# Linformer attention and maxout FFN: batch 0 loaded by casting DMAs of one queue, first FFN chunk begun with half of the features

## Chip, cores, metric

One core of a Trainium2 chip. The metric is device time in microseconds (us). "Span" is the time from the first to the last instruction in a profile or a timed execution. It is 2.1 to 2.2 us shorter than the time for the kernel before and about 1.8 us shorter for the changed one. I compare times with times and spans with spans.

In the profile lines PE is TensorE, PEld its weight loads, DVE is VectorE, ACT ScalarE, POOL GpSimd, SP the engine that issues the plain loads. A timeline line gives start and duration in us, the engine, the line of the kernel, the tiles written and read with their shapes, and the count; in brackets stands how long the engine was idle before it and what ended that wait. The granted clock is TensorE's clock as a share of full speed.

## The reference, cut to what matters

```python
k_proj = einsum('ks,bhsd->bhkd', E, k);  v_proj = einsum('ks,bhsd->bhkd', F, v)
attn   = softmax(q @ k_proj.T / 8)               # b=8 batches, 8 heads, s=1024, d=64, k=64
x      = (attn @ v_proj) -> [8192, 512]          # heads side by side
h      = max(x @ w1, x @ w2, x @ w3)             # 512 -> 768
out    = h @ w_out                               # 768 -> 512
```

All inputs are fp32 in HBM; the kernel computes in bf16 with fp32 sums.

## The kernel before

Heads go in four pairs ("pair g"). Each pair of batch 0 gives 128 of the 512 features of x. The FFN runs in chunks of 512 tokens. TensorE's order is fixed by the program; `bank()` and `two()` deal one PSUM bank or two neighbouring ones of eight, the one that the program's own clock thinks free first; `idle(n)` issues filler matmuls.

Batch 0 comes as fp32 over the SP queue, is cast on DVE and ACT, and the weights follow on the GpSimd queue, held back by casts:

```python
    load_q(0); load_k(0); load_k(1); load_q(1)                # nc.sync, fp32 tiles q_f, k_f
    for (a, b), t in zip([(0, 4), (4, 6), (6, 8)], v_f):
        nc.sync.dma_start(out=t, in_=view(v, 0)[:, a:b])
    ...
    cast_k(2, "v")
    load_w(0, 0, cast_k(3, "v"))                              # w1, features 0-255, after this cast
    ...                                                       # (cut: pairs 0 to 3)
    cast_v(2, "v"); cast_v(3, "s")
    v_pair(1)
    scale_x(0, 0, *C0, values(0, 0, *C0))
    ...
    v_pair(3)
    idle(1)
```

The first FFN chunk keeps six sums of w1 in six PSUM banks, then takes w2 and w3:

```python
        for i in range(3):
            ...
            if i == 0:    # features 0-127 of all six, 128-255, then 256-511; pair 3's values inside
                parts = [(A, (0,)), (Bq, (0,)), (A, (1,)), (Bq, (1,)), (A, (2, 3)), (Bq, (2, 3))]
            else:
                parts = [(A, (0, 1)), (A, (2, 3)), (Bq, (0, 1)), (Bq, (2, 3))]
            ...
                        if i == 0:
                            copy("sv"[jt % 2], hs[:, jt], t, ns)          # w1 to SBUF
                        else:
                            most(hs[:, jt] if i == 1 else hTs[0, 0][:, jt, :], t, ns, hs[:, jt])
```

The softmax here doesn't subtract the row's maximum and nothing guards it: scores larger than these inputs give would overflow.

Of the kernel before, what the change touches and what calls it, by code (L numbers as in the profile page):

```python
# [15 lines left out]
def kernel(  # L16
# [21 lines left out]
    P = 128  # L38
# [98 lines left out]
    first_ctx = ExitStack()  # L137
    first = first_ctx.enter_context(tc.tile_pool(name="first", bufs=1))

    ef_f = first.tile([P, S], FP32, name="ef_f")  # L140
    ef_b = first.tile([P, S], BF16, name="ef_b")
    q_f = [first.tile([P, 4, SPC, D], FP32, name=f"q_f{i}") for i in range(2)]
    k_f = [first.tile([P, 4, SI, D], FP32, name=f"k_f{i}") for i in range(2)]
    k_c = [first.tile([P, SI, 2, D], BF16, name=f"k_c{g}") for g in range(NPAIR)]
    q_c = [first.tile([P, 2, SPC, 2, D], BF16, name=f"q_c{i}") for i in range(2)]
    v_heads = [(0, 4), (4, 6), (6, 8)]
    v_f = [first.tile([P, b - a, SI, D], FP32, name=f"v_f{a}") for a, b in v_heads]
# [3 lines left out]
    def load_q(i):  # L151
        nc.sync.dma_start(out=q_f[i], in_=view(q, 0)[:, 4 * i:4 * i + 4, 0:SPC])  # L152

    def load_k(i):
        nc.sync.dma_start(out=k_f[i], in_=view(k, 0)[:, 4 * i:4 * i + 4])

    load_q(0)
    load_k(0)
    load_k(1)
    load_q(1)  # L160
    for (a, b), t in zip(v_heads, v_f):
        nc.sync.dma_start(out=t, in_=view(v, 0)[:, a:b])  # L162
# [6 lines left out]
    def load_w(i, half, earlier=None):  # L169
        cts = slice(half * NCT // 2, (half + 1) * NCT // 2)  # L170
        w = (moe_w1, moe_w2, moe_w3)[i].rearrange("(ct p) j -> p ct j", p=P)
        dma = nc.gpsimd.dma_start(out=w_sb[i][:, cts, :], in_=w[:, cts, :])
        if earlier is not None:
            after(dma, earlier)

    def load(b):
        tiles = tuple(
            loads.tile([P, H, SI, D], BF16, name=nm) for nm in ("q_t", "k_t", "v_t")
        )
        qkv[b] = tiles  # L180
        for i in ((1, 0, 2) if b == 1 else (0, 1, 2)):
            dma = nc.gpsimd.dma_start(out=tiles[i], in_=view((q, k, v)[i], b))  # L182
            if i == 0 and b - 1 in last_T:
                after(dma, last_T[b - 1])



# [140 lines left out]
    LO, HI = slice(0, H // 2), slice(H // 2, H)  # L328

# [63 lines left out]
    def cast_q(g, eng):  # L393
        copy(
            eng, q_c[g // 2][:, g % 2].rearrange("p si h d -> p h si d"),
            q_f[g // 2][:, 2 * (g % 2):2 * (g % 2) + 2],
        )

    def turn_q(g):
        t, ns = two()  # L400
        t = t.bitcast(BF16)[:, 0]
        for si in range(SPC):
            nc.tensor.transpose(
                out=t[:, si * P:(si + 1) * P],
                in_=q_c[g // 2][:, g % 2, si].rearrange("p h d -> p (h d)"),
                identity=ident,
            )
        pe(0.3)
        copy(
            "v", qTs[0][:, g * SI:g * SI + SPC, :].rearrange("a si p -> a (si p)"),  # L410
            t[:, 0:CHUNK], ns, 0.43,
        )

    def cast_k(g, eng):
        return copy(
            eng, k_c[g].rearrange("p si h d -> p h si d"),
            k_f[g // 2][:, 2 * (g % 2):2 * (g % 2) + 2], (), 0.7,
        )

    def k_pair(g):  # L420

        t, ns = bank()
        for si in range(SI):
            nc.tensor.matmul(
                out=t[:, 0:KP], lhsT=k_c[g][:, si].rearrange("p h d -> p (h d)"),
                rhs=efT[:, si, 0, :], start=(si == 0), stop=(si == SI - 1),
            )
        pe(0.5)
        copy("v", kpTs[0][:, g, :], t[:, 0:KP], ns, 0.25)

    def cast_v(g, eng):
        a = (0, 0, 4, 6)[g]
        return copy(
            eng, v_t[:, 2 * g:2 * g + 2],
            v_f[max(0, g - 1)][:, 2 * g - a:2 * g - a + 2], (), 0.7,
        )
# [6 lines left out]

    C0 = (0, SPC)
    idle(11)
    turn_ef()
    cast_q(0, "v")
    cast_q(1, "s")
    idle(3)
    turn_q(0)  # L450
    turn_q(1)
    idle(6)
    cast_k(0, "v")
    cast_k(1, "s")
    k_pair(0)
    idle(1)
    k_pair(1)
    sc01 = [scores(0, 0, *C0)]
    exps(0, 0, *C0, sc01[0])
    idle(1)  # L460
    sc01.append(scores(0, 1, *C0))
    exps(0, 1, *C0, sc01[1])
    idle(1)
    z01 = [sums(0, 0, *C0)]
    idle(1)
    invert(0, 0, *C0, z01[0])
    cast_k(2, "v")
    load_w(0, 0, cast_k(3, "v"))
    k_pair(2)
    z01.append(sums(0, 1, *C0))  # L470
    invert(0, 1, *C0, z01[1])
    cast_q(2, "v")
    k_pair(3)
    cast_q(3, "v")
    turn_q(2)
    turn_q(3)
    sc23 = [scores(0, g, *C0) for g in (2, 3)]
    for g in (2, 3):
        exps(0, g, *C0, sc23[g - 2])
    idle(3)  # L480
    load_w(0, 1, cast_v(0, "v"))
    load_w(1, 0)
    load_w(1, 1)
    load_w(2, 0)
# [41 lines left out]
    def up_first(work):  # L526
# [5 lines left out]
        for i in range(3):  # L532
# [8 lines left out]
            for n, (jts, cts) in enumerate(parts):  # L541
                for jt in jts:
                    if h[jt] is None:
                        h[jt] = bank()
# [200 lines left out]
```

## Time and profile before

| | before |
|---|---|
| time, first runs | 408.73, 408.83, 408.86 and 410.6 us |
| span of the profiled execution | 409.1 us, mean granted clock 0.994 |
| TensorE busy | 395.4 us, 97% |
| first FFN matmul | 23.74 us |
| first matmul of the down projection | 43.04 us |

TensorE is the bound from about 25 us on. The interesting part is the head: what TensorE waits for until then. I use the first down matmul as a mark; everything ahead of it is "the head". The prediction shows the lines.

### The profile page before, as it was taken

What the parts mean: (1) busy time and instruction counts of PE and PEld (TensorE: products, weight loads), DVE (VectorE), ACT (ScalarE), POOL (GpSimd) and SP (SyncE); (2) the same over time, 40 slices, a digit from 0 to 9 for tenths busy, and PEclk for the clock granted to TensorE, in tenths of its full rate; (3) what the DMA queues carried; (4) which work ended last, traced back from release to release, by engine and by line L of the source; (5) the groups of instructions that cost most, each with busy time, mean ns of one, the idle gap of its engine ahead of it and who ended that gap; (6) DMA issues with size and microseconds to landing.
All of it is one profiled execution on the core that took longest, in us unless ns stands there. A gap on an engine that the chain in (4) does not pass through costs nothing.

```text
span 409.1 us, 6066 instructions
## 1 busy us (share of the span) xinstructions
PE 395.4 (97%) x2415; PEld 181.1 (44%) x2459; DVE 205.8 (50%) x319; ACT 194.2 (47%) x281; POOL 25.3 (6%) x35
## 2 busy tenths in 40 slices
PE   7889999999999999999999999999999999999995
PEld 3534444345444544444544445444544444444443
DVE  2737655464474526636463564525465363525251
ACT  3721527722764266457435555536545556432322
POOL 0421002002000200200110002000000000000000
PEclk9989999999999999999999999999999999999999
DMA  8999948958935994596699108970440202020202
GB/s 263 353 207 204 183 132 123 229 154 123 244 55 129 211 229 128 87 226 124 183 185 198 53 0 225 200 194 0 66 142 2 103 0 104 0 105 0 104 0 103
DMA packets 58475, 54.91 MB, mean 134 GB/s; under 512 B 25936, under 2 KB 52048, under 8 KB 58448
## 3 DMA queue, kind: packets, MB, share of 16 engines
q0 software_dynamic: 25296, 25.69, 39.4%
q1 hardware_dynamic: 33008, 28.71, 21.6%
q8 instruction: 19, 0.31, 0.3%
q10 hardware_dynamic: 144, 0.13, 0.1%
q14 instruction: 8, 0.07, 0.1%
HBM read 57.15 MB, written 16.78 MB: 181 GB/s over the span
## 4 chain that ended last, share of the span: by engine, by line
PE 90%; DMA 4%; SPq 2%; ACT 1%; issue 1%; DVE 1%; DVEq 0%
PE banks L513 60%; PE banks L611 19%; PE banks L216 4%; PE banks L277 3%; DMA v_f<-in_v_dram 3%; PE banks L196 2%; SPq L162 1%; PE banks L288 1%; DMA out_dram<-o_sb 0%; DVE m L576 0%; DVE xT L246 0%; ACT o_sb L99 0%; SPq L152 0%; ACT zi L235 0%; ACT v_t L99 0%
## 5 line engine op out<-in xcount | busy, mean ns | idle before, releaser
L513 PE MATMUL banks<-xT,w_sb 128*128 128x512 bf16 x1118 | 254.7, 380 | 2.1 <-issue 0.6
L513 PEld LDWEIGHTS <-w_sb 128*128 128x128 bf16 x1152 | 109.9, 98 | 137.6 <-issue 10.9
L576 DVE TENSOR_TENSOR m<-banks,h1s 128x512 f32<-128x512 f32 x90 | 62.1, 690 | 86.3 <-ACT h1s L572 54.7
L572 ACT COPY h1s<-banks 128x512 f32<-128x512 f32 x90 | 52.5, 583 | 92.8 <-PE banks L513 89.6
L611 PE MATMUL banks<-wout_sb,hT 128*128 128x512 bf16 x370 | 84.8, 379 | 0.9 <-issue 0.3
L246 DVE TENSOR_TENSOR xT<-banks,zi 128x1024 bf16<-128x1024 f32 (+1 forms) x36 | 39.7, 1106 | 77.2 <-ACT zi L235 57.4
L523 DVE TENSOR_TENSOR hT<-banks,m 128x512 bf16<-128x512 f32 x90 | 62.3, 692 | 9.4
L99 ACT COPY o_sb<-banks 128x512 f32<-128x512 f32 (+1 forms) x60 | 34.9, 581 | 53.0 <-PE banks L611 53.0
L611 PEld LDWEIGHTS <-hT 128*128 128x128 bf16 x378 | 36.1, 98 | 45.5 <-DVE hT L523 2.9
L229 ACT ACTIVATE zl<-banks 128x1024 f32<-128x1024 f32 (+1 forms) x36 | 33.5, 930 | 31.7 <-PE banks L216 31.6
L207 ACT ACTIVATE pT<-banks 128x1024 bf16<-128x1024 f32 (+1 forms) x36 | 33.4, 932 | 9.9 <-PE banks L196 9.0
L235 ACT ACTIVATE zi<-zl 128x1024 f32<-128x1024 f32 (+1 forms) x36 | 34.6, 962 | 1.1
L182 POOL DMA_DIRECT2D q_t<-in_q_dram x7 | 6.2, 880 | 208.9 <-DMA qT<-q_p 61.5
L277 PEld LDWEIGHTS <-efT 128*64 128x64 bf16 x288 | 14.0, 113 | 5.2 <-issue 4.7
L216 PE MATMUL banks<-pT,ones 64*64 64x512 bf16 (+1 forms) x144 | 13.9, 376 | 0.8 <-DVE xT L246 0.3
L196 PE MATMUL banks<-qT,kpT 64*64 64x512 bf16 (+1 forms) x144 | 13.4, 360 | 0.9 <-DVE m L576 0.3
L216 PE MATMUL banks<-pT,vp 64*64 64x512 bf16 (+1 forms) x144 | 13.4, 359 | 0.2 <-DVE vp L99 0.2
L277 PE MATMUL banks<-v_t,efT 128*64 128x256 bf16 (+1 forms) x176 | 10.3, 262 | 2.0 <-ACT v_t L99 2.0
L372 PE MATMUL banks<-warm 128*128 128x512 bf16 x29 | 10.1, 469 | 1.2 <-DVE warm L165 1.2
L216 PEld LDWEIGHTS <-ones 64*64 64x64 bf16 x144 | 4.3, 103 | 14.9 <-issue 14.7
L99 DVE CAST vp<-banks 64x256 bf16<-64x256 f32 (+1 forms) x18 | 7.1, 396 | 6.0 <-ACT vp L99 3.4
L99 ACT CAST vp<-banks 64x256 bf16<-64x256 f32 x14 | 5.1, 365 | 7.3 <-PE banks L277 7.1
(50 smaller groups left out, 104.5 us busy)
## 6 DMA issues: line engine op xcount, KB each, us to landing
out_dram<-o_sb SPq DMA_DIRECT2D x30, 512.0 KB, 3.6
k_t<-in_k_dram POOLq DMA_DIRECT2D x7, 1024.0 KB, 14.5
q_t<-in_q_dram POOLq DMA_DIRECT2D x7, 1024.0 KB, 9.4
v_t<-in_v_dram POOLq DMA_DIRECT2D x7, 1024.0 KB, 18.6
w_sb<-in_moe_w_dram POOLq DMA_DIRECT2D x6, 384.0 KB, 8.5
k_f<-in_k_dram SPq DMA_DIRECT2D x2, 1024.0 KB, 7.9
q_f<-in_q_dram SPq DMA_DIRECT2D x2, 512.0 KB, 7.2
v_f<-in_v_dram SPq DMA_DIRECT2D x1, 1024.0 KB, 11.6
```

Of the source, the lines that this page charges most:

```text
L99: done = {"v": nc.vector.tensor_copy, "s": nc.scalar.copy, "g": nc.gpsimd.tensor_copy}[eng](out=o, in_=i)
L207: nc.scalar.activation(out=pTs[b, g, lo], in_=t, func=AF.Exp, scale=scale)
L216: nc.tensor.matmul(out=t[hp * HALF:(hp + 1) * HALF, c, 0:nsi * HALF], lhsT=w(rows, hp), rhs=p[rows, hp, :], start=True, stop=True,)
L229: nc.scalar.activation(out=zl, in_=t, func=AF.Ln)
L235: nc.scalar.activation(out=zi, in_=zl, func=AF.Exp, scale=-1.0)
L246: nc.vector.tensor_tensor(out=xTs[b][:, g, lo:lo + nsi, :].rearrange("a (c s) p -> a c (s p)", c=2), in0=t, in1=zi, op=ALU.mult,)
L277: nc.tensor.matmul(out=t[hh * HALF:(hh + 1) * HALF, 0:width], lhsT=efT[:, si, kv - 1, :], rhs=qkv[b][kv][:, heads[hh], si, :], start=(si = ...
L513: nc.tensor.matmul(out=h, lhsT=w_sb[i][:, ct, jt * P:(jt + 1) * P], rhs=xTs[b][:, ct, ch * SPC:(ch + 1) * SPC, :], start=(ct == 0), stop=( ...
L523: nc.vector.tensor_tensor(out=o, in0=h, in1=other, op=ALU.max)
L572: nc.scalar.copy(out=h1s, in_=h[0][0])
L576: nc.vector.tensor_tensor(out=m12, in0=h[1][0], in1=h1s, op=ALU.max)
L611: nc.tensor.matmul(out=o_ps, lhsT=hTs[b, ch][:, jt, tt * P:(tt + 1) * P], rhs=wout_sb[:, jt, :], start=(jt == 0), stop=(jt == NJT - 1),)
```

## The change

The intent is to start the FFN earlier. All of batch 0 comes as bf16 through casting DMAs of the GpSimd queue, nearly in the order of need, so the casts go. When only pairs 0 and 1 are done, the FFN begins with features 0 to 255: w1's half sums are copied to SBUF (s1), w2's half sums stay open in six PSUM banks. Pairs 2 and 3 are computed as one "duo" in between. Then come the second halves; w1's is added to s1 on GpSimd.

```diff
-    load_q(0); load_k(0); load_k(1); load_q(1)      # nc.sync, fp32, then casts
+    load_q(LO, slice(0, SPC)); load_kv(1, LO)       # nc.gpsimd, fp32 -> bf16
+    load_kv(2, slice(0, 2));   load_kv(2, slice(2, 4))
+    load_w(0, 0)
+    load_q(HI, slice(0, SPC)); load_kv(1, HI)
+    load_w(1, 0)
+    load_kv(2, V2); load_kv(2, V3)
+    load_w(1, 1); load_w(0, 1); load_w(2, 0); load_w(2, 1)
 ...
+        h = six()
+        for ct in range(2):
+            for jt in jts:
+                up_mm(h[jt][0], 0, 0, 0, jt, (ct,), last=1)      # w1, features 0-255
+                if ct == 1:
+                    copy("sv"[jt % 2], s1[:, jt], *h[jt])
+        then(0)                                                 # q, k, exp, sums of pairs 2, 3
+        load_k1()
+        h = six()
+        for ct in range(2):
+            for jt in jts:
+                up_mm(h[jt][0], 1, 0, 0, jt, (ct,))             # w2, features 0-255, stay in PSUM
+        then(2)                    # v_pair(2), x_pairs(1, (0,)), v_pair(3), x_pairs(1, (1,))
+        for jt in jts:
+            t, ns = bank()
+            up_mm(t, 0, 0, 0, jt, (2, 3), first=2)
+            copy("s", s2[:, jt], t, ns)
+            nc.gpsimd.tensor_tensor(out=s1[:, jt], in0=s1[:, jt], in1=s2[:, jt], op=ALU.add)
+            up_mm(h[jt][0], 1, 0, 0, jt, (2, 3))
+            most(s1[:, jt], *h[jt], s1[:, jt], added)
+        for jt in jts:
+            ...                                                 # w3, all features, then max into hT
 ... (cut: duo versions of transposes, scores, exp, sums, values; plan of the work between)
```

More of the change, by code (lines that the diff above doesn't have):

```diff
@@ L135, with load_kv, load_q, load_w @@
     qkv[0] = (q_t, k_t, v_t)
-    first_ctx = ExitStack()
-    first = first_ctx.enter_context(tc.tile_pool(name="first", bufs=1))
-    ef_f = first.tile([P, S], FP32, name="ef_f")
-    ef_b = first.tile([P, S], BF16, name="ef_b")
-    q_f = [first.tile([P, 4, SPC, D], FP32, name=f"q_f{i}") for i in range(2)]
-    k_f = [first.tile([P, 4, SI, D], FP32, name=f"k_f{i}") for i in range(2)]
-    k_c = [first.tile([P, SI, 2, D], BF16, name=f"k_c{g}") for g in range(NPAIR)]
-    q_c = [first.tile([P, 2, SPC, 2, D], BF16, name=f"q_c{i}") for i in range(2)]
-    v_heads = [(0, 4), (4, 6), (6, 8)]
-    v_f = [first.tile([P, b - a, SI, D], FP32, name=f"v_f{a}") for a, b in v_heads]
+    ef_f = const.tile([P, S], FP32, name="ef_f")
+    ef_b = const.tile([P, S], BF16, name="ef_b")
     nc.sync.dma_start(out=ef_f[0:KP], in_=E)
     nc.sync.dma_start(out=ef_f[KP:P], in_=F)
-    def load_q(i):
-        nc.sync.dma_start(out=q_f[i], in_=view(q, 0)[:, 4 * i:4 * i + 4, 0:SPC])
-    def load_k(i):
-        nc.sync.dma_start(out=k_f[i], in_=view(k, 0)[:, 4 * i:4 * i + 4])
-    load_q(0)
-    load_k(0)
-    load_k(1)
-    load_q(1)
-    for (a, b), t in zip(v_heads, v_f):
-        nc.sync.dma_start(out=t, in_=view(v, 0)[:, a:b])
+    def load_kv(i, heads):
+        nc.gpsimd.dma_start(
+            out=qkv[0][i][:, heads], in_=view((q, k, v)[i], 0)[:, heads]
+        )
+    def load_q(heads, sis):
+        nc.gpsimd.dma_start(
+            out=q_t[:, heads, sis], in_=view(q, 0)[:, heads, sis]
+        )
+    def load_w(i, half):
+        cts = slice(half * NCT // 2, (half + 1) * NCT // 2)
+        w = (moe_w1, moe_w2, moe_w3)[i].rearrange("(ct p) j -> p ct j", p=P)
+        nc.gpsimd.dma_start(out=w_sb[i][:, cts, :], in_=w[:, cts, :])
+    LO, HI, ALL = slice(0, H // 2), slice(H // 2, H), slice(0, H)
+    V2, V3 = slice(4, 6), slice(6, 8)
+    load_q(LO, slice(0, SPC))
+    load_kv(1, LO)
+    load_kv(2, slice(0, 2))
+    load_kv(2, slice(2, 4))
     nc.scalar.preload_act_table_set("natural_log_exp_and_others")
@@ L167, with load_k1 @@
     nc.vector.memset(ones, 1.0)
-    def load_w(i, half, earlier=None):
-        cts = slice(half * NCT // 2, (half + 1) * NCT // 2)
-        w = (moe_w1, moe_w2, moe_w3)[i].rearrange("(ct p) j -> p ct j", p=P)
-        dma = nc.gpsimd.dma_start(out=w_sb[i][:, cts, :], in_=w[:, cts, :])
-        if earlier is not None:
-            after(dma, earlier)
+    load_w(0, 0)
+    load_q(HI, slice(0, SPC))
+    load_kv(1, HI)
+    load_w(1, 0)
+    load_kv(2, V2)
+    load_kv(2, V3)
+    load_w(1, 1)
+    load_w(0, 1)
+    load_w(2, 0)
+    load_w(2, 1)
+    load_q(ALL, slice(SPC, SI))
+    nc.gpsimd.dma_start(out=wout_sb, in_=moe_w_out.rearrange("(jt p) m -> p jt m", p=P))
+    def load_k1():
+        nonlocal k_t1
+        k_t1 = loads.tile([P, H, SI, D], BF16, name="k_t")
+        nc.gpsimd.dma_start(out=k_t1, in_=view(k, 1))
+    k_t1 = None
     def load(b):
         tiles = tuple(
-            loads.tile([P, H, SI, D], BF16, name=nm) for nm in ("q_t", "k_t", "v_t")
+            loads.tile([P, H, SI, D], BF16, name=nm) if b > 1 or i != 1 else k_t1
+            for i, nm in enumerate(("q_t", "k_t", "v_t"))
         )
         qkv[b] = tiles
-        for i in ((1, 0, 2) if b == 1 else (0, 1, 2)):
+        for i in ((0, 2) if b == 1 else (0, 1, 2)):
             dma = nc.gpsimd.dma_start(out=tiles[i], in_=view((q, k, v)[i], b))
@@ L327 @@
     kps = {}
-    LO, HI = slice(0, H // 2), slice(H // 2, H)
     def kproj(b):
@@ L391, in turn_ef @@
             )
-    def cast_q(g, eng):
-        copy(
-            eng, q_c[g // 2][:, g % 2].rearrange("p si h d -> p h si d"),
-            q_f[g // 2][:, 2 * (g % 2):2 * (g % 2) + 2],
-        )
-    def turn_q(g):
-        t, ns = two()
-        t = t.bitcast(BF16)[:, 0]
-        for si in range(SPC):
-            nc.tensor.transpose(
-                out=t[:, si * P:(si + 1) * P],
-                in_=q_c[g // 2][:, g % 2, si].rearrange("p h d -> p (h d)"),
-                identity=ident,
-            )
-        pe(0.3)
-        copy(
-            "v", qTs[0][:, g * SI:g * SI + SPC, :].rearrange("a si p -> a (si p)"),
-            t[:, 0:CHUNK], ns, 0.43,
-        )
-    def cast_k(g, eng):
-        return copy(
-            eng, k_c[g].rearrange("p si h d -> p h si d"),
-            k_f[g // 2][:, 2 * (g % 2):2 * (g % 2) + 2], (), 0.7,
-        )
     def k_pair(g):
@@ L423, in k_pair @@
         for si in range(SI):
-            nc.tensor.matmul(
-                out=t[:, 0:KP], lhsT=k_c[g][:, si].rearrange("p h d -> p (h d)"),
-                rhs=efT[:, si, 0, :], start=(si == 0), stop=(si == SI - 1),
-            )
-        pe(0.5)
-        copy("v", kpTs[0][:, g, :], t[:, 0:KP], ns, 0.25)
-    def cast_v(g, eng):
-        a = (0, 0, 4, 6)[g]
-        return copy(
-            eng, v_t[:, 2 * g:2 * g + 2],
-            v_f[max(0, g - 1)][:, 2 * g - a:2 * g - a + 2], (), 0.7,
-        )
+            for hp in range(2):
+                nc.tensor.matmul(
+                    out=t[hp * HALF:(hp + 1) * HALF, 0:KP],
+                    lhsT=k_t[:, 2 * g + hp, si, :],
+                    rhs=efT[:, si, 0, :], start=(si == 0), stop=(si == SI - 1),
+                )
+        pe(0.45)
+        copy("v", kpTs[0][:, g, :], t[:, 0:KP], ns, 0.25)
     def v_pair(g):
@@ L442, in v_pair, with q_duo @@
         copy("v", vps[0][:, hs].rearrange("a h d -> a (h d)"), t[:, 0:2 * D], ns, 0.3)
+    def q_duo(u):
+        t, ns = bank()
+        t = t.bitcast(BF16)
+        for gg in range(2):
+            heads_q(0, 2 * u + gg, range(SPC), t[:, gg * CHUNK:(gg + 1) * CHUNK])
+        o = qTs[0].rearrange("a (g si) p -> a g si p", si=SI)
+        copy(
+            "v", o[:, 2 * u:2 * u + 2, 0:SPC, :],
+            t.rearrange("a (g si p) -> a g si p", si=SPC, p=P), ns, 0.7,
+        )
+    N0 = SPC * HALF
@@ new lines, in sc_duo @@
+    def sc_duo(u):
+        t, ns = two()
+        for gg in range(2):
+            g = 2 * u + gg
+            for c in range(2):
+                for hp in range(2):
+                    rows = slice(hp * HALF, (hp + 1) * HALF)
+                    at = g * SI + c * SPC // 2
+                    nc.tensor.matmul(
+                        out=t[c * HALF:(c + 1) * HALF, hp, gg * N0:(gg + 1) * N0],
+                        lhsT=kpTs[0][rows, g, :],
+                        rhs=qTs[0][rows, at:at + SPC // 2, :],
+                        start=True, stop=True,
+                    )
+        return t, ns, pe(0.5)
@@ new lines, in exp_duo, with sum_duo @@
+    def exp_duo(u, sc):
+        t, ns, ready = sc
+        pTs[0, u] = att.tile([P, 2, CHUNK], BF16, name="pT", bufs=4)
+        nc.scalar.activation(out=pTs[0, u], in_=t, func=AF.Exp, scale=scale)
+        runs("s", ready, 1.0, ns)
+    def sum_duo(u):
+        t, ns = two()
+        for c in range(2):
+            rows = slice(c * HALF, (c + 1) * HALF)
+            for hp in range(2):
+                nc.tensor.matmul(
+                    out=t[hp * HALF:(hp + 1) * HALF, c],
+                    lhsT=ones[rows], rhs=pTs[0, u][rows, hp, :],
+                    start=True, stop=True,
+                )
+        ready = pe(0.25)
+        zl = att.tile([P, 2, CHUNK], FP32, name="zl", bufs=1)
+        nc.scalar.activation(out=zl, in_=t, func=AF.Ln)
+        runs("s", ready, 1.0, ns)
+        zi = att.tile([P, 2, CHUNK], FP32, name="zi", bufs=2)
+        nc.scalar.activation(out=zi, in_=zl, func=AF.Exp, scale=-1.0)
+        zis[0, u] = zi, runs("s", ready, 1.0)
@@ new lines, in x_pairs @@
+    def x_pairs(u, pairs):
+        t, ns = two()
+        for i, gg in enumerate(pairs):
+            for c in range(2):
+                rows = slice(c * HALF, (c + 1) * HALF)
+                for hp in range(2):
+                    nc.tensor.matmul(
+                        out=t[hp * HALF:(hp + 1) * HALF, c, i * N0:(i + 1) * N0],
+                        lhsT=vps[0][rows, 2 * (2 * u + gg) + hp, :],
+                        rhs=pTs[0, u][rows, hp, gg * N0:(gg + 1) * N0],
+                        start=True, stop=True,
+                    )
+        ready = pe(0.15 * len(pairs))
+        zi, when = zis[0, u]
+        for i, gg in enumerate(pairs):
+            g = 2 * u + gg
+            nc.vector.tensor_tensor(
+                out=xTs[0][:, g, 0:SPC, :].rearrange("a (c s) p -> a c (s p)", c=2),
+                in0=t[:, :, i * N0:(i + 1) * N0],
+                in1=zi[:, :, gg * N0:(gg + 1) * N0],
+                op=ALU.mult,
+            )
+            runs("v", max(ready, when), 0.69, ns)
@@ L446, with up_mm @@
     turn_ef()
-    cast_q(0, "v")
-    cast_q(1, "s")
-    idle(3)
-    turn_q(0)
-    turn_q(1)
+    q_duo(0)
     idle(6)
-    cast_k(0, "v")
-    cast_k(1, "s")
     k_pair(0)
-    idle(1)
-    k_pair(1)
-    sc01 = [scores(0, 0, *C0)]
-    exps(0, 0, *C0, sc01[0])
-    idle(1)
-    sc01.append(scores(0, 1, *C0))
-    exps(0, 1, *C0, sc01[1])
-    idle(1)
-    z01 = [sums(0, 0, *C0)]
-    idle(1)
-    invert(0, 0, *C0, z01[0])
-    cast_k(2, "v")
-    load_w(0, 0, cast_k(3, "v"))
-    k_pair(2)
-    z01.append(sums(0, 1, *C0))
-    invert(0, 1, *C0, z01[1])
-    cast_q(2, "v")
-    k_pair(3)
-    cast_q(3, "v")
-    turn_q(2)
-    turn_q(3)
-    sc23 = [scores(0, g, *C0) for g in (2, 3)]
-    for g in (2, 3):
-        exps(0, g, *C0, sc23[g - 2])
-    idle(3)
-    load_w(0, 1, cast_v(0, "v"))
-    load_w(1, 0)
-    load_w(1, 1)
-    load_w(2, 0)
-    nc.gpsimd.dma_start(out=q_t[:, :, SPC:], in_=view(q, 0)[:, :, SPC:])
-    load_w(2, 1)
-    nc.gpsimd.dma_start(out=wout_sb, in_=moe_w_out.rearrange("(jt p) m -> p jt m", p=P))
-    cast_v(1, "v")
-    z23 = [sums(0, 2, *C0)]
-    invert(0, 2, *C0, z23[0])
-    v_pair(0)
-    z23.append(sums(0, 3, *C0))
-    invert(0, 3, *C0, z23[1])
-    cast_v(2, "v")
-    cast_v(3, "s")
-    v_pair(1)
-    scale_x(0, 0, *C0, values(0, 0, *C0))
-    idle(1)
-    scale_x(0, 1, *C0, values(0, 1, *C0))
-    v_pair(2)
-    idle(2)
-    scale_x(0, 2, *C0, values(0, 2, *C0))
-    v_pair(3)
-    idle(1)
-    first_ctx.close()
+    k_pair(1)
+    for g in range(2):
+        exps(0, g, *C0, scores(0, g, *C0))
+    z01 = []
+    for g in range(2):
+        idle(2)
+        z01.append(sums(0, g, *C0))
+        invert(0, g, *C0, z01[g])
+        v_pair(g)
+    idle(1)
+    for g in range(2):
+        scale_x(0, g, *C0, values(0, g, *C0))
     ffn_sb = ctx.enter_context(tc.tile_pool(name="ffn_sb", bufs=2))
     hTs = {}
-    def up_mm(h, i, b, ch, jt, cts):
+    def up_mm(h, i, b, ch, jt, cts, first=0, last=NCT - 1):
         for ct in cts:
@@ L516, in up_mm @@
                 rhs=xTs[b][:, ct, ch * SPC:(ch + 1) * SPC, :],
-                start=(ct == 0),
-                stop=(ct == NCT - 1),
+                start=(ct == first),
+                stop=(ct == last),
             )
@@ L526, in up_first @@
     def up_first(work):
-        hs = ffn_sb.tile([P, NJT, CHUNK], FP32, name="hs", bufs=1)
-        hTs[0, 0] = ffn_sb.tile([P, NJT, CHUNK], BF16, name="hT")
-        A, Bq = (0, 1, 2), (3, 4, 5)
-        for i in range(3):
-            if i == 0:
-                h = [(t[:, n], ns[n:n + 1]) for t, ns in (two(), two(), two()) for n in (0, 1)]
-            else:
-                h = [None] * NJT
-            if i == 0:
-                parts = [(A, (0,)), (Bq, (0,)), (A, (1,)), (Bq, (1,)), (A, (2, 3)), (Bq, (2, 3))]
-            else:
-                parts = [(A, (0, 1)), (A, (2, 3)), (Bq, (0, 1)), (Bq, (2, 3))]
-            for n, (jts, cts) in enumerate(parts):
-                for jt in jts:
-                    if h[jt] is None:
-                        h[jt] = bank()
-                    up_mm(h[jt][0], i, 0, 0, jt, cts)
-                    if cts[-1] == NCT - 1:
-                        t, ns = h[jt]
-                        if i == 0:
-                            copy("sv"[jt % 2], hs[:, jt], t, ns)
-                        else:
-                            most(
-                                hs[:, jt] if i == 1 else hTs[0, 0][:, jt, :], t, ns, hs[:, jt]
-                            )
-                run_later()
-                for f in work.get((i, n), []):
-                    f()
@@ new lines, in then, with six @@
+        def then(key):
+            run_later()
+            for f in work.get(key, []):
+                f()
+        s1 = ffn_sb.tile([P, NJT, CHUNK], FP32, name="s1", bufs=1)
+        s2 = ffn_sb.tile([P, NJT, CHUNK], FP32, name="s2", bufs=1)
+        hTs[0, 0] = ffn_sb.tile([P, NJT, CHUNK], BF16, name="hT")
+        jts = range(NJT)
+        def six():
+            return [(t[:, n], ns[n:n + 1]) for t, ns in (two(), two(), two()) for n in (0, 1)]
+        h = six()
[4 more added lines that the diff above has]
+                    copy("sv"[jt % 2], s1[:, jt], *h[jt])
@@ new lines, in up_first @@
+        then(0)
[6 more added lines that the diff above has]
+        for jt in jts:
+            t, ns = bank()
+            up_mm(t, 0, 0, 0, jt, (2, 3), first=2)
+            copy("s", s2[:, jt], t, ns)
+            nc.gpsimd.tensor_tensor(out=s1[:, jt], in0=s1[:, jt], in1=s2[:, jt], op=ALU.add)
+            added = clock["s"] + 1.2
+            up_mm(h[jt][0], 1, 0, 0, jt, (2, 3))
+            most(s1[:, jt], *h[jt], s1[:, jt], added)
@@ L558, in up @@
+        then(4)
+        for jt in jts:
+            t, ns = bank()
+            up_mm(t, 2, 0, 0, jt, range(NCT))
+            most(hTs[0, 0][:, jt, :], t, ns, s1[:, jt])
+            then(5 + jt)
     def up(b, ch, jt):
@@ L698, with attend @@
                 c1 = (SPC, SPC)
+                def attend(u):
+                    exp_duo(u, sc_duo(u))
                 up_first({
-                    (0, 0): [lambda: scale_x(0, 3, *C0, values(0, 3, *C0))],
-                    (1, 3): [qp(0, (0, 1), *c1)],
-                    (2, 0): [qp(0, (2, 3), *c1), sc(0, 0, *c1)],
-                    (2, 1): [sc(0, 1, *c1)],
-                    (2, 3): [za(0, 0, *c1), sc(0, 2, *c1)],
+                    0: [lambda: q_duo(1), lambda: k_pair(2), lambda: k_pair(3),
+                        lambda: attend(1), lambda: idle(3), lambda: sum_duo(1)],
+                    2: [lambda: v_pair(2), lambda: x_pairs(1, (0,)),
+                        lambda: v_pair(3), lambda: x_pairs(1, (1,))],
+                    5: [qp(0, (0, 1), *c1)],
+                    6: [qp(0, (2, 3), *c1)],
+                    7: [sc(0, 0, *c1)],
+                    8: [sc(0, 1, *c1)],
+                    10: [za(0, 0, *c1), sc(0, 2, *c1)],
                 })
```

## The prediction

> **What bounds the kernel now.** I read the page's 40 slices first: TensorE is busy nine tenths or more nearly everywhere, so a gain must come out of slots where it is busy with filler or waiting. Then the windows, to see which slots these are.
>
> ```profile
> 0.00:5.00 5.00, 3.81 (x9) 1.34 (x10) 0.35 (x2) 1.28 (x1) 0.70 (x6) 1.00 0.58 134
> 5.00:10.00 5.00, 3.71 (x27) 1.85 (x26) 2.47 (x6) 2.23 (x4) 0.00 (x0) 1.00 1.06 386
> 10.00:15.00 5.00, 4.45 (x65) 2.62 (x64) 3.38 (x11) 4.06 (x7) 0.88 (x1) 1.00 1.06 395
> 15.00:20.00 5.00, 4.52 (x77) 2.44 (x74) 4.27 (x9) 3.70 (x7) 3.05 (x5) 1.00 1.10 325
> 20.00:25.00 5.00, 2.96 (x24) 1.47 (x24) 0.98 (x2) 1.04 (x1) 3.14 (x4) 0.72 1.15 209
> 25.00:30.00 5.00, 5.00 (x26) 2.23 (x26) 1.97 (x3) 1.32 (x3) 0.00 (x0) 0.94 1.30 202
> 30.00:35.00 5.00, 4.95 (x24) 2.25 (x23) 3.09 (x6) 0.43 (x1) 0.00 (x0) 1.00 1.22 208
> ...
> 50.00:409.00 359.00, 351.35 (x2046) 160.54 (x2084) 178.87 (x267) 173.08 (x248) 15.78 (x18) 1.00 0.55 119
> ```
>
> Columns: stretch, its length, busy time of PE, PEld, DVE, ACT, POOL, then granted clock, DMA share, GB/s. From 25 us on PE is full, and stays so (351 of 359 us after 50); in 20 to 25 it is busy 2.96 of 5 us, and the clock falls to 0.72. Then the chain of work that ended last:
>
> ```profile
> 8.44 12.79 DMA v_f<-in_v_dram
> 21.23 0.02 issue
> 21.25 1.05 ACT v_t L99
> 22.30 0.04 issue
> 22.34 1.06 PE banks L277 x16
> 23.41 0.54 PE banks L372
> 23.95 1.28 PE banks L513 x3
> ```
>
> Everything hangs on the last piece of v (heads 6 and 7), which lands at 21.2 us; then a cast, its projection, and the first FFN matmul at 23.74. From there the chain is PE alone to the end. So this is two problems: a head of some 25 us set by loads and by dependent small steps, and 384 us of PE work, which the change hardly touches. The timeline gives the mark to compare with: the first down matmul starts at 43.04.
>
> ```profile
> 43.04 1.46 PE L611 MATMUL banks<-wout_sb,hT 128*128 128x512 bf16 x6
> ```
>
> **What the Trainium skill says.** (1) "DMA: Bandwidth & Descriptors", section "Issuing engines are not separate DMA queues": all queues share the same 16 engines, so a cast on another queue is not free bandwidth. The trace agrees: with v still loading, the third v piece took 12.8 us once weights went in beside it. (2) "GPSIMD Engine Reference", section 3.1: a fp32 tensor_tensor add of 2048 elements measured 4497 ns on GpSimd, about 2.6 cycles an element. For 512 elements that is an estimate of 1.1 to 1.2 us; no such add runs in this trace (the DVE's of that size take 690 ns). (3) "SBUF — State Buffer", section "Who interferes with whom": a DVE instruction with one SBUF input does not contend with GpSimd. The DVE maxima here read PSUM and one SBUF tile, so I charge nothing; this trace cannot show it. (4) "TensorE: Matmul & The Clock Gate", Part 1: idle windows of about 3.4 us halve the clock. The trace has such a drop (0.72) around the 2.01 us wait before 22.34.
>
> **The change, part by part.**
>
> *Loads.* Fp32 loads moved about 400 GB/s (windows); casting loads write about 208 GB/s of bf16, which is 416 GB/s read. Per input element they cost the same, so the total DMA time does not shrink; the order changes. Counting fp32 bytes read (E and F 0.52 MB, q low heads 0.52, k low 1.05, v pairs 0.52 each, a half weight 0.79), before had k's first half in at 9.42 us (issue 2.62 plus 6.8) after 2.1 MB. After needs the same 2.1 MB for it. The software queue starts slower (an isolated q load at 93.55 took 9.3 us for what is 5.0 us at rate), but it starts beside E and F, which ran at 218 GB/s only. I take 9.4 us for k low and 0.416 MB per 1 us onwards: w1 first half about 14 us, k high 18, w2 first half 20, v4-5 and v6-7 21.4 and 22.6, w2 second half 24.5, w1 second half 26.4, w3 28 to 30, wout 36.5. The built program makes the ninth software DMA wait for the first to land, the tenth for the second; seven stay outstanding, so I charge nothing.
>
> *Casts removed.* Twelve casts on DVE and ACT go (q 0.42, k and v 0.69 each on DVE, 1.05 on ACT); with them the wait cast-then-PE ahead of k, q and v.
>
> *Chain from k low to the first FFN matmul.* Two k projections of 16 small matmuls, 0.55 each as an estimate from the v projection's 0.57 to 0.64; kpT copy 0.23; scores 0.25; two exps 0.59; sums; ln 0.60 and exp 0.63 twice; the scale 0.69: k pair from 9.45, exp at 10.9 to 12.1, ln and inverse of pair 0 to 13.4, of pair 1 to 14.7, xT pair 0 ready 15.3. First FFN matmul about 15.4 instead of 23.74; its 12 matmuls (220 ns each in the steady rows) end at 18.0.
>
> *Pairs 2 and 3 inside the FFN.* q transposes 0.6, the qT copy 0.69 behind three DVE copies of s1 (ready 19.9), scores, one exp of 1.04, sums: PE gets to w2 at 22.3 and ends it at 24.95. Then v pair 2, its copy, values, scale, and only then v pair 3: the open w2 sums hold six banks, so all four share the last two banks, and the built program shows v pair 3 and the first w1 matmul waiting for DVE. Each round is 0.64 + 0.35 + 0.30 + 0.80 = 2.1 us, of which PE works 0.9; the second w1 half starts at 29.05. About 2.4 us of new PE wait.
>
> *The add and the maxima.* w1 and w2 second halves: 24 matmuls, 5.3 us, to 34.3. Each s1+s2 goes PE, ACT copy 0.59, GpSimd add 1.2, DVE max 0.69. First add starts at 30.2, the sixth ends at 37.4, the DVE max at 38.1. DVE then does hT and qT (0.69 each, in order), so the scores of chunk 1 get qT at 39.5, while PE could be there at 38.1: 1.4 us of wait. After them come 0.3 + 0.9 + 0.3 + 1.8 + 0.7 us of matmuls: down starts near 43.5.
>
> *Sum.* 43.5 against 43.04: +0.5 us. The 8.3 us won at the start of the FFN go to pairs 2 and 3 (some 6 us with their own waits, formerly ahead of the FFN), the bank round (2.4) and the add chain (1.4); the cold stretch at 22 to 25 us, about 1.3 us by its longer matmuls, is saved. What follows is the same matmuls.
>
> **The rivals.**
>
> A: loads set the head. If software DMAs start 1 us later than I take, k low lands at 10.4 and all of it moves: 410.3. For it: the isolated load's slow start. Against: weights issued at 16.95 landed in 6.8 us beside others. If they start earlier (two queues at once), 408.3.
>
> B: no new waits. If the bank round and the add chain hide better, PE is the bound from 15.4 on; 3.8 us come back: 405.5. Against: the order of the built program shows the waits.
>
> C: the GpSimd add is slower, 1.6 us in place of 1.2: six adds are 2.4 us later, and DVE passes it all on: 411.7. Nothing in the profile speaks to it.
>
> D: the clock drops in the bank round (PE is busy 1.9 of 4.1 us from 25 to 29), costing about what it cost before, 1.3 us: 410.6.
>
> E: the next batch's loads come late. k of batch 1 must now wait for batch 0's k tile; it lands near 41 us as an estimate and is used at 50. Free.
>
> **Range and chances.** The sum gives 408.86 + 0.5 = 409.4. My landing time and roundings lean late more than early, so I say 409.0. The named errors are 1 to 3 us each, of both signs: 406.0 to 411.8 for 8 in 10. Two per cent is 8.2 us: to win it the whole head advance would have to survive, to lose it three rivals would have to add up. Faster 0.02, within 2% 0.97, slower 0.01.
>
> **What would show it.** Right: the first FFN matmul near 15 to 16.5 us; PE waits on DVE ahead of v pair 3 and of the second w1 half; GpSimd adds about 1.2 us apart and PE waiting on qT in the third weight; first down matmul at 42.5 to 45. Wrong: if FFN work from 16 us on runs with no waits of 0.5 us or more, the time is near 405; if k low lands past 11 us or adds are 1.6 us apart, it is 411 or more. If the first down matmul moves but the end does not move with it, my claim that the rest is unchanged fails.

## The result, and the profile after

411.62 us (411.41 to 412.83) against 408.85: 0.6% slower, inside the 2% that the prediction held most likely; ratio 1.0064, interval 1.0037 to 1.0091. Ratios here are the mean time of one kernel's fast runs over that of the other's of the same rounds, so they differ a little from the quotient of the medians. Every execution here and below counts as undisturbed.

The first view is the changed kernel's windows (columns as in the prediction), where the head used to end and after.

```profile
10.00:15.00 5.00, 4.15 (x61) 2.17 (x64) 1.87 (x5) 3.48 (x6) 2.14 (x3) 1.00 1.26 204
...
20.00:25.00 5.00, 4.17 (x38) 1.83 (x36) 0.29 (x1) 2.85 (x3) 1.70 (x2) 1.00 1.18 210
25.00:30.00 5.00, 2.73 (x28) 1.49 (x30) 1.68 (x3) 0.58 (x1) 0.04 (x1) 0.75 1.23 204
30.00:35.00 5.00, 5.00 (x23) 2.17 (x22) 2.08 (x3) 2.84 (x5) 4.55 (x4) 0.91 1.31 205
35.00:40.00 5.00, 3.95 (x47) 1.93 (x46) 3.50 (x6) 0.08 (x1) 4.64 (x5) 1.00 1.25 206
...
50.00:409.00 359.00, 351.99 (x2049) 160.71 (x2086) 179.01 (x268) 173.50 (x249) 15.76 (x18) 1.00 0.55 119
```

The hole of 20 to 25 us (2.96 of 5 us busy) is filled. A hole of the same depth now stands at 25 to 30 us (2.73), with its own clock drop (0.75), and a second one at 35 to 40 (3.95). The long last row is as before, 351.99 against 351.35. The timeline names the waits, in brackets:

```profile
14.59 2.75 PE L522 MATMUL banks<-xT,w_sb 128*128 128x512 bf16 x11 [0.66 <-DVE xT L257]
...
24.96 0.30 PE L480 MATMUL banks<-pT,vp 64*64 64x256 bf16 x4 [0.46 <-DVE vp L99]
...
26.13 0.64 PE L288 MATMUL banks<-v_t,efT 128*64 128x128 bf16 x16 [0.87 <-DVE xT L490]
...
27.15 0.30 PE L480 MATMUL banks<-pT,vp 64*64 64x256 bf16 x4 [0.38 <-DVE vp L99]
...
28.25 0.58 PE L522 MATMUL banks<-xT,w_sb 128*128 128x512 bf16 x1 [0.80 <-DVE xT L490]
29.05 6.70 PE L522 MATMUL banks<-xT,w_sb 128*128 128x512 bf16 x26 [0.22 <-issue]
...
31.67 6.18 POOL L568 TENSOR_TENSOR s<-s,s 128x512 f32<-128x512 f32 x5 [0.45 <-ACT s L99]
...
39.83 0.30 PE L207 MATMUL banks<-qT,kpT 64*64 64x256 bf16 x4 [1.00 <-DVE qT L99]
...
43.55 1.47 PE L632 MATMUL banks<-wout_sb,hT 128*128 128x512 bf16 x6
```

The first FFN matmul comes at 14.59 in place of 23.74 us, 9 us earlier, and the first down matmul at 43.55 in place of 43.04. Four waits of 0.46, 0.87, 0.38 and 0.80 us lie in the bank round of v pairs 2 and 3 (2.5 us). Five GpSimd adds take 6.18 us, so they come 1.24 us apart, and the scores of chunk 1 wait 1.00 us for a qT copy, which stands on DVE behind the last of the maxima that need these adds. After the mark the two kernels run 409.1 - 43.04 = 366.1 and 409.9 - 43.55 = 366.35 us. The span is about 1.8 us shorter than the time for the changed kernel.

So the two profiles differ by 0.8 us, much as predicted, but the times by 2.8 us. That gap was the first question of the experiments.

### The profile page after: what moved, and what is told of

It reads as the page before. It is cut to its first block, busy times and chain, and to the rows that moved or that the text cites. A ratio compares the mean times of both kernels' runs of the same rounds, so it can differ in the third digit from the quotient of the medians.

```text
span 409.9 us, 6124 instructions
## 1 busy us (share of the span) xinstructions
PE 394.5 (96%) x2452; PEld 180.5 (44%) x2497; DVE 200.9 (49%) x308; ACT 194.1 (47%) x281; POOL 38.6 (9%) x49
## 4 chain that ended last, share of the span: by engine, by line
PE 91%; DVE 3%; ACT 2%; DMA 2%; issue 1%; SPq 0%; DVEq 0%; ACTq 0%
PE banks L522 60%; PE banks L632 19%; PE banks L227 4%; PE banks L288 4%; PE banks L207 2%; DMA ef_f<-in_F_dram 1%; PE banks L299 1%; PE banks L381 1%; DMA out_dram<-o_sb 0%; DVE xT L257 0%; DVE s L99 0%; ACT zl L240 0%; ACT pT L218 0%; DVE xT L490 0%; DVE m L597 0%
## 5 line engine op out<-in xcount | busy, mean ns | idle before, releaser
L257 DVE TENSOR_TENSOR xT<-banks,zi 128x1024 bf16<-128x1024 f32 (+1 forms) x34 | 38.3, 1130 | 75.3 <-ACT zi L246 57.7
L240 ACT ACTIVATE zl<-banks 128x1024 f32<-128x1024 f32 (+1 forms) x34 | 32.3, 949 | 30.5 <-PE banks L227 30.2
L218 ACT ACTIVATE pT<-banks 128x1024 bf16<-128x1024 f32 (+1 forms) x34 | 32.1, 951 | 7.6 <-PE banks L207 7.6
L246 ACT ACTIVATE zi<-zl 128x1024 f32<-128x1024 f32 (+1 forms) x34 | 33.4, 981 | 1.1
L207 PE MATMUL banks<-qT,kpT 64*64 64x512 bf16 (+1 forms) x136 | 12.7, 364 | 1.4 <-DVE qT L99 1.0
L99 ACT COPY s<-banks 128x512 f32<-128x512 f32 x9 | 5.1, 588 | 10.5 <-remote 5.9
L381 PE MATMUL banks<-warm 128*128 128x512 bf16 x23 | 8.3, 501 | 1.5 <-DVE warm L165 1.2
```

What stands on the lines that cost most here:

```text
L99: done = {"v": nc.vector.tensor_copy, "s": nc.scalar.copy, "g": nc.gpsimd.tensor_copy}[eng](out=o, in_=i)
L218: nc.scalar.activation(out=pTs[b, g, lo], in_=t, func=AF.Exp, scale=scale)
L240: nc.scalar.activation(out=zl, in_=t, func=AF.Ln)
L246: nc.scalar.activation(out=zi, in_=zl, func=AF.Exp, scale=-1.0)
L257: nc.vector.tensor_tensor(out=xTs[b][:, g, lo:lo + nsi, :].rearrange("a (c s) p -> a c (s p)", c=2), in0=t, in1=zi, op=ALU.mult,)
```

## The experiments

Twelve runs, each timed over five rounds, on several chips. Kernels are compared only within the same rounds.

**1. The kernel before, again.** No edit.

> The kernel before, unchanged, for a second profile. Theory 1 (the page of before that the prediction used is of one of its slow-clock executions: its runs differ by 1.8 us, and the cold stretch at 20 to 25 us costs about that): 408.8 us, clock 0.999 to 1.0 in most executions and 0.995 or so in the 410.6 kind, and a profile of the first kind has the first down matmul near 41.4 us, not at 43.04. Rival (the heads are equal within 0.5 us as the two pages say, and the 2.7 us arise later): first down matmul at 43.0 again, and the stretch from there to the end 2 us shorter than the 366.4 us of the changed kernel.

Measured: 409.85 us (before: 409.48; ratio 1.001, interval 0.9992 to 1.0027). All 17 executions of this code had a clock of 0.998 to 1.0 and spans of 406.4 to 408.4 us. The profiled page with its 409.1 us at 0.994 is outside that. Below are 2 us windows, first of the page used for the prediction:

```profile
20.00:22.00 2.00, 0.30 (x4) 0.22 (x5) 0.69 (x1) 0.75 (x1) 2.00 (x3) 1.00 1.16 210
22.00:24.00 2.00, 1.66 (x18) 1.10 (x18) 0.29 (x1) 0.29 (x1) 1.14 (x2) 0.55 1.16 209
24.00:26.00 2.00, 2.00 (x10) 0.54 (x9) 0.29 (x1) 0.00 (x0) 0.00 (x0) 0.60 1.16 209
```

then of the second profile of the same kernel:

```profile
20.00:22.00 2.00, 1.64 (x26) 0.92 (x27) 1.51 (x4) 1.31 (x3) 2.00 (x3) 1.00 0.94 134
22.00:24.00 2.00, 1.32 (x20) 0.78 (x19) 0.96 (x2) 0.63 (x1) 2.00 (x4) 1.00 1.14 199
24.00:26.00 2.00, 2.00 (x14) 0.84 (x13) 0.69 (x1) 0.00 (x0) 0.68 (x1) 1.00 1.16 207
```

and its timeline:

```profile
22.68 0.64 PE L277 MATMUL banks<-v_t,efT 128*64 128x128 bf16 x16 [0.82 <-ACT v_t L99]
...
41.96 1.46 PE L611 MATMUL banks<-wout_sb,hT 128*128 128x512 bf16 x6
```

In the page the clock was 0.55 and 0.60 just where the FFN begins; in the second profile it stayed at 1.00, and its first down matmul is at 41.96 us. From the end of the last v cast to that mark it took 20.7 us in the page (22.30 to 43.04) and 19.3 us in the second (22.64 to 41.96): the drop cost 1.4 us. From the mark to the end both take 366.0 to 366.1 us. The theory holds for the page. It fails for the spread of the rest: executions at clock 0.998 to 1.0 still differ by up to 2 us. The loads vary: k's first half landed at 9.4 us in the page and at 11.0 us here (on another chip). How much of the spread this explains I did not settle.

**2. Without the adds** (wrong result).

```diff
-            nc.gpsimd.tensor_tensor(out=s1[:, jt], in0=s1[:, jt], in1=s2[:, jt], op=ALU.add)
```

> The changed kernel without the six GpSimd adds; the copies of the second half stay, the result is wrong on purpose. If the add chain is on the path (DVE maxima 1.24 us apart, PE waiting 1.0 us for qT at 38.8): that wait goes, the first down matmul comes 1.0 to 1.4 us earlier, about 410.4 us. If the adds are hidden anyway: within 0.3 us of 411.6.

Measured: 411.65 us, so by the median no gain: the expected 410.4 was missed. But there are two kinds of executions: span 408.0 and 408.1 us at clock 1.0, and 409.9 to 410.0 at 0.994 to 0.996. The profiled one is of the second kind:

```profile
21.96 0.41 PE L460 MATMUL banks<-pT,ones 64*64 64x512 bf16 x4 [0.37 <-ACT pT L452]
...
30.19 6.79 PE L522 MATMUL banks<-xT,w_sb 128*128 128x512 bf16 x26 [0.22 <-issue]
...
39.98 0.30 PE L207 MATMUL banks<-qT,kpT 64*64 64x256 bf16 x4
...
43.70 1.47 PE L631 MATMUL banks<-wout_sb,hT 128*128 128x512 bf16 x6
```

The wait ahead of the scores (line L207) is gone. From the sums of pairs 2 and 3 (L460) to the mark it took 21.74 us, against 22.72 in the changed kernel (20.83 to 43.55): the chain is worth 1.0 us even with a clock drop, whose 26 matmuls took 6.79 us. The two kinds of this run lie 1.9 us apart. The slow matmuls of the profile account for some 1.4 us of that (7.5 us from 29.38 to 36.90, where run 3 below takes 6.15 for the same stretch at full clock); the rest was not taken apart. The changed kernel, whose first four executions lay at 409.6 and 409.8 us (clock 0.999 and 1.0) and at 409.9 and 411.1 us (0.996), shows less of a drop: there the adds partly hide it. Its wait for qT is 1.00 us with a drop, and 1.40 in run 3 without one.

**3. v projections of pairs 2 and 3 among the first w2 matmuls.**

```diff
         for ct in range(2):
             for jt in jts:
+                if (ct, jt) == (1, 0): v_pair(2)
+                if (ct, jt) == (1, 3): v_pair(3)
                 up_mm(h[jt][0], 1, 0, 0, jt, (ct,))
-        2: [v_pair(2), x_pairs(1, (0,)), v_pair(3), x_pairs(1, (1,))]
+        2: [x_pairs(1, (0, 1))]
```

> The changed kernel with the v projections of pairs 2 and 3 put between the first w2 matmuls, and one round of values for both pairs. If the bank round's waits (0.46 + 0.87 + 0.38 + 0.80 = 2.5 us of idle PE) set the end: the second half of w1 starts about 26.6 us (its weights land at 26.55) in place of 28.25, and all later work moves with it, 1.5 us: about 410.1 us, and the clock stays at 1.0. If the add chain is the only bound after it, the same, as the chain starts from that matmul. If the time lies elsewhere: 411.6.

Measured: 410.02 us, ratio to before 1.0021 (1.0007 to 1.0035). Clock 0.999 to 1.0 in all six executions. The timeline:

```profile
27.45 6.22 PE L522 MATMUL banks<-xT,w_sb 128*128 128x512 bf16 x28 [1.52 <-DMA w_sb<-in_moe_w_dram]
...
38.15 0.30 PE L207 MATMUL banks<-qT,kpT 64*64 64x256 bf16 x4 [1.40 <-DVE qT L99]
...
41.88 1.47 PE L636 MATMUL banks<-wout_sb,hT 128*128 128x512 bf16 x5
```

The bank round was part of the loss: the mark moves to 41.88 us. The start was 27.45 and not 26.6, since a new wait took the place of the old, 1.52 us for the weights of w1's second half. The add chain then shows its full 1.40 us. The clock stayed at 1.00 although PE was busy only 0.55 of the 2 us from 26 to 28, so a sparse stretch does not always bring a drop. The changed kernel itself was not timed in runs 2 to 5, and the interval here overlaps that of run 11, so these runs rest on their traces more than on their ratios.

**4. Three of the six adds on DVE, straight from PSUM.**

```diff
+            if jt % 2:
+                nc.vector.tensor_tensor(out=s1[:, jt], in0=t, in1=s1[:, jt], op=ALU.add)
+            else:          # ACT copy and GpSimd add as before; maxima of jt - 1 and jt after the DVE add
```

> The changed kernel with three of the six adds done by DVE straight from PSUM (no copy, no GpSimd), the other three on GpSimd as before. DVE then has nine operations of 0.69 us in place of six waiting on adds 1.24 us apart: the last maximum ends about 1.7 us earlier and PE's 1.0 us wait for qT goes. Add chain on the path: about 410.5 us, correct result. Add chain hidden: 411.6. DVE the new bound: slower than 411.6.

Measured: 410.19 us, ratio 1.0027 (1.0011 to 1.0042), result correct. PE no longer waits for qT (its scores start at 37.72 us in the profile, with no wait) and the mark is at 41.45. The clock still drops in some executions (0.993 and 0.994 at the two longest spans, 409.8 and 409.0; the rest 407.8 to 408.4).

**5. Both, and w1's second half loaded ahead of w2's.**

> The changed kernel with both waits shortened at once (v projections among the first w2 matmuls, three of six adds on DVE), and the second half of w1 loaded ahead of that of w2, because v_early showed PE waiting 1.52 us for it. If the two waits are what the changed kernel lost: w1's second half starts near 26 us, no wait for qT, first down matmul about 40 us against 43.55, span 406.3 to 406.8 us, some 1 us faster than the kernel before. If the two overlap (one hides the other): no better than v_early or split, span 408.

Measured: 409.19 us against 409.3, ratio 1.0002 (0.9986 to 1.0018); spans 406.7 to 408.6. The timeline:

```profile
27.59 6.20 PE L522 MATMUL banks<-xT,w_sb 128*128 128x512 bf16 x28 [1.47 <-DVE xT L490]
...
40.52 1.47 PE L642 MATMUL banks<-wout_sb,hT 128*128 128x512 bf16 x6
```

The two gains add up, but the expected lead over the kernel before did not come. w1's second half started at 27.59 us, not near 26: one more wait, 1.47 us, for DVE to scale both pairs. The sums of pairs 2 and 3 (L460) start at different times with the loads, so the stretch from there to the mark is what compares best. It is 22.72 us in the changed kernel with its clock drop; without the drop I estimate 21.85 us, from the 7.42 us measured up to w1's second half and the 14.43 us that run 3 took from there to the mark. It is 20.74 us in run 3, 20.36 in run 4 and 19.20 here. So the bank round is worth about 1.1 us and the add chain about 1.5.

**6. The loads alone.** Casting DMAs of one queue and no casts, but the first FFN chunk as before: all of v ahead of w1. The transposes of q go in duos here too, and the fillers are set anew, with four fewer.

```diff
+    load_q(LO, ...); load_kv(1, LO); load_kv(1, HI); load_q(HI, ...)
+    load_kv(2, LO); load_kv(2, slice(4, 6)); load_kv(2, slice(6, 8))
+    load_w(0, 0); load_w(0, 1); load_w(1, 0); ...
-    (all casts)                                  # up_first() unchanged
```

> One part of the change alone: batch 0 by casting DMAs of one queue, without the DVE and ACT casts, but the first FFN chunk as in the kernel before (all of v ahead of w1 in the queue). With the landing times of the changed kernel (0.37 MB per us from 2.1 MB at 8.9 us) v is complete near 18.7 us and w1's first half near 21: the FFN starts at about 21 in place of 23.5 and its first down matmul at 39.5 to 40: span about 405.5, 1.5 to 2 us faster than before. If casting DMAs are themselves the loss (slower start, slower packets): FFN start at 23.5 or later and the time as before or slower.

Measured: 408.66 us against 409.3, ratio 0.9997 (0.9978 to 1.0016). Two kinds again: spans 406.2 to 406.4 at clock 1.0, and 407.3 to 408.2 at 0.992 to 0.996. The profile, of the first kind:

```profile
21.68 0.82 PE L468 MATMUL banks<-xT,w_sb 128*128 128x512 bf16 x3 [0.38 <-DMA w_sb<-in_moe_w_dram]
...
40.17 1.46 PE L566 MATMUL banks<-wout_sb,hT 128*128 128x512 bf16 x6
```

The FFN starts 7 us later than in the changed kernel and the mark comes 3.4 us earlier, of which some 0.9 is the clock drop in the changed kernel's profile. The expected 21 us was 21.68, and 405.5 was too low by 0.7 even for the fastest execution.

**7. As 6, with w1's first half ahead of v's last four heads** and 12 FFN matmuls ahead of their values, all in PSUM.

> As loads_only, but w1's first half ahead of the last four v heads in the queue and the FFN's first 12 matmuls ahead of their values, all in PSUM (no SBUF copy, no add). The FFN starts near 18.5 us but must wait for w1's second half, which lands near 23: gain over loads_only 0.5 us at most, span 405 to 405.7. If the loads set the end of the head and not the order of the matmuls, loads_only and this one are equal.

Measured: 408.91 us, ratio 0.9991 (0.9974 to 1.0009), spans 406.1 to 406.5 at clock 1.0 and 407.7 to 407.9 at 0.996. The FFN started at 18.89 us; the mark is at 40.07. It is equal to number 6 within the spread, and the expected 405 to 405.7 was too low: starting earlier gave nothing by itself.

**8. Filler matmuls in the changed kernel's bank round.**

```diff
-        2: [v_pair(2), x_pairs(1, (0,)), v_pair(3), x_pairs(1, (1,))]
+        2: [v_pair(2), idle(2), x_pairs(1, (0,)), v_pair(3), idle(2), x_pairs(1, (1,))]
```

> The changed kernel with two filler matmuls beside each vp copy of the bank round (0.44 us each time, in a wait of 0.46 and 0.38 us), so that TensorE is busier there. If the clock drop of the changed kernel costs nothing because the add chain hides it: clock 0.998 to 1.0 in every execution and the span still 409.5 to 409.9 us. If the drop is part of its loss: span about 408.

Measured: 411.73 us, ratio 1.0042 (1.0016 to 1.0067). Five of six executions at clock 0.999 to 1.0, spans 409.4 to 410.2; one at 0.996, 410.6. So most of the loss is there without a drop: the five at full clock have a mean span of 409.8 us, those of the kernel before 407.6. (The fillers did not stop every drop.)

**9 and 10. Numbers 6 and 7 with filler matmuls in their waits.** In number 9 `idle(6)` before k became `idle(8)`, and `idle` of 2, 1, 3 and 2 more went after the first sums, around the q transposes and ahead of the FFN. Number 10 has those but the last (eight fillers, not the six that its expectation names).

> loads_only with ten more filler matmuls in the waits that its profile shows (before k, after the sums, around the q transposes, before the FFN). loads_only had two kinds of executions, 406.2 to 406.4 us at clock 1.0 and 407.3 to 408.2 at 0.992 to 0.996. If the clock drop is what parts them: all at 406.2 to 406.6 us, about 0.3% faster than the kernel before. If the fillers delay real work: all near 407.

> loads_w1 with six more filler matmuls in the same waits. Same question: all executions at 406.1 to 406.6 us if the clock parts them, with no 407.7 to 407.9 kind; near 407 if the fillers delay real work.

Measured: 408.95 us against 409.77, ratio 0.9972 (0.9946 to 0.9998), clock 0.998 to 1.0, spans 406.5 to 407.8; and 409.19, ratio 0.9974 (0.9947 to 1.0002), clock 0.997 to 1.0. The clock drops of 0.992 to 0.996 are gone, and the kind at 407.7 to 408.2 nearly so. That all would lie at 406.2 to 406.6 was wrong, but the chip was another one, with the kernel before at 406.9 to 408.3 and one execution at 410.9 (clock 0.996). Without that one the gain of number 9 is 0.2%. The kernel before with more fillers was not run, so what the fillers alone give is not shown.

**11. The changed kernel again, and 12. number 9 again**, side by side.

> The changed kernel, unchanged, with more rounds and beside the next run. If the result of the first four executions holds: 1.005 to 1.0075 of the kernel before, span 409.5 to 410 us whatever the clock (0.996 or 1.0).

> loads_only_warm unchanged, a repeat for a closer interval, since the first was taken against a kernel before with one execution at 412.99 us. If the gain is real: ratio 0.997 to 0.9985 with an interval below 1. If it came of that one execution: 0.999 to 1.0.

Measured: the changed kernel 412.2 against 410.88, ratio 1.0036 (1.0008 to 1.0064). Spans 409.0 to 411.3: of the two at clock 1.0, 409.0 and 409.9; of those at 0.990 to 0.996, 409.7 to 411.3. So "whatever the clock" was too strong; the adds hide only part of a drop. Number 9: 409.07, ratio 0.9959 (0.9932 to 0.9985): faster than both kernels. In the chain of waits of this profile of the changed kernel the adds stand themselves (in the first profile the chain names PE ahead of the last maximum, which started at 37.89 us, 0.04 us after the last add):

```profile
31.63 0.59 ACT s L99
...
32.30 1.26 POOL s L568
...
33.99 1.87 POOL s L568 x2
...
37.67 1.28 POOL s L568
...
39.59 0.68 DVE hT L532
40.27 0.61 DVE qT L99
40.88 0.04 issue
40.92 0.30 PE banks L207 x4
```

## Why the prediction was right, and where its centre was off

The range (406.0 to 411.8) held 411.62, near its upper end; the centre, 409.0, was 2.6 us low.

*Loads and casts.* k's first half was taken to land at 9.4 us and landed at 8.9. The first FFN matmul was predicted at 15.4 and came at 14.59. In the two timed comparisons with fillers, runs 9 and 12, this part alone is a gain of 0.3 and 0.4%; some 0.35 us of it (0.1%) is the smaller gap between time and span. Run 6, without the fillers, shows it only in its executions at clock 1.0. Of the 12.8 us that the prediction gives for the third v piece most is the queue ahead of it; the sharing with the weights shows in the 3.9 us between the landing of the second piece (17.3) and of the third (21.2), for 0.52 MB that would take 1.3 us at 0.4 MB per us.

*Bank round.* Predicted 2.4 us of waits, and w1's second half at 29.05; measured 2.5 us and 28.25.

*Add chain.* Predicted 1.2 us an add, 1.4 us of wait, scores at 39.5; measured 1.24, 1.0 and 39.83. The maxima kept their 0.69 us beside the running adds, as the prediction assumed. The clock drop beside the chain (rival D) came, and part of it is inside these figures: it slowed the matmuls ahead of the adds. A clock below 0.998 stands in 6 of the 10 timed executions of the changed kernel (this result and run 11), and in 3 of 50 of the kernel before.

*Mark.* Predicted 43.5, measured 43.55. The closeness is luck in part: w1's second half started 0.8 us early, its 28 matmuls took 1.3 us longer at the low clock (7.44 against 6.15 us in run 3), and the wait for qT was 0.4 shorter.

*The term that was mis-sized* is the other side of the subtraction: "43.5 against 43.04: +0.5 us", and the sum "408.86 + 0.5". 43.04 us is the mark of one execution of 409.1 us of span, by the gap of 2.1 to 2.2 us some 411.2 us of time, with a clock drop; the difference to it was added to 408.86, the time of another kind of execution. Added to its own 411.2 it would have given 411.7. I even saw the drop: the sum counts "the cold stretch at 22 to 25 us, about 1.3 us by its longer matmuls, is saved".

But a usual run of the kernel before has no such stretch to save. Its clock is 0.998 to 1.0, and with 366.05 us after the mark the spans of 406.4 to 408.4 us in run 1 (mean 407.3) put its mark between 40.4 and 42.4, at 41.3 in the mean. For the executions near 408.8 us the same working gives about 40.6, an estimate. Against that the changed kernel's 43.55 is 2.9 us late; with 0.3 us more after the mark and 0.35 us less between span and time that agrees with the 2.8 us timed. Of the 2.4 us between 43.04 and 40.6 the 1.4 us of the drop are shown; the remaining 1.0 I put to the spread of loads and chips, which I did not take apart. The prediction's own signs tell the same: for 411 us or more it asked for k past 11 us or adds 1.6 us apart, and neither came.

*Rivals.* A (late loads) did not happen in the first profile, where k came earlier; in run 11's profile k's first half landed at 10.4 us, the FFN began at 15.85 and the mark is 44.64. C (slow adds) fell: 1.24 us. B, that without the two new waits PE would be the bound from 15 us on and 405.5 us the time, was tried by run 5: the waits go, a new one comes (1.47 us for DVE's scaling; in run 3 it was 1.52 us for weights), and the kernel only draws level. E held: k of batch 1 landed at 41.9 us and was used at 50.7, and from the mark to the end the two profiles differ by 0.3 us.

So the gain went into waits inside the FFN. The change starts the FFN 9 us earlier with 24 matmuls of 0.22 us, 5.3 us of work, and holds six of eight banks while pairs 2 and 3 go through the other two one after another; then it pays six adds of 1.24 us on GpSimd, ahead of DVE maxima of 0.69 us. Runs 6 and 7 show that casting loads without this start do better, and run 12 shows it: 409.07 us against the changed kernel's 412.2.

That low use of TensorE lets its clock fall is what the Trainium skill says in "TensorE: Matmul & The Clock Gate", Part 1. The traces agree in kind: the clock fell to 0.50 after the sparse stretches in the page of before, in the changed kernel, and in run 2. In runs 3 and 5 waits of 1.52 and 1.47 us passed without a drop, so these runs do not say what exactly brings one.

## What to carry to other kernels

Before adding a difference read from a profile to a timed median, check that the profiled execution is a usual one: compare its span and clock with the timed runs, and treat a clock drop as a property of that execution. An earlier start is worth only what the same resources can keep running: here six PSUM banks held open left two for everything that had to come next. Test a change of several parts by its parts; one of these was a gain and the other a larger loss.

## What the Trainium skill lacked or had wrong

- "TensorE: Matmul & The Clock Gate", Part 1, warns of idle gaps longer than about 3.4 us. Here the clock fell to 0.50 to 0.55 after a single wait of 2.0 us (page of before), and in the changed kernel with no wait over 0.87 us, after 4 us in which PE was busy 1.74 us. In run 3 a wait of 1.52 us left it at 1.00. Its section on a second failure mode names such micro-idling, without a figure.
- "DMA: Bandwidth & Descriptors" says that casting needs the GpSimd queue but gives no rate. Loads casting fp32 to bf16 wrote 204 to 210 GB/s, which is about 410 GB/s read, close to the 386 to 395 GB/s of the plain loads.
- "GPSIMD Engine Reference", section 3.1, has the add only at 2048 elements. At 512 elements it took 1.26 us, the next starting 1.24 us later; 1.1 to 1.2 had been estimated from the page.
- No page that I read says why the time exceeds the span by 2.1 to 2.2 us in one kernel and 1.8 us in the other.
